# Attention and SwiGLU on one core: q, k and x turned on TensorE in all eight batches, stores issued from ScalarE's queue

## The chip, the core and the metric

The program runs on one core of one Trainium2 chip. The metric is the device time in microseconds (us); the lower the better. Five engines run beside each other, each through its own list of instructions in order: PE (TensorE, matrix products and transposes), DVE (VectorE), ACT (ScalarE), POOL (GpSimd) and SP (SyncE, which here only issues transfers). ACT and POOL can issue transfers too. DMA engines move the data.

## What is computed

For 8 batches with 8 heads, 576 tokens and head dimension 64, causal attention with a decay from a "forget" input f, and then an RMS norm and a SwiGLU feed-forward network over the 4608 tokens:

```
scores = q @ k.T / sqrt(64) + cum[:, None] - cum[None, :]      # cum = cumsum(log(clip(f)))
attn   = softmax(causal(scores));   x = attn @ v               # x: 4608 x 512, all heads side by side
xn     = x / sqrt(mean(x*x) + 1e-6) * rms_g
out    = (silu(xn @ w_gate) * (xn @ w_val)) @ w_out            # 512 -> 1536 -> 512
```

All inputs and the output are float32; the kernel works on bf16 copies of the matrix operands.

## The kernel before

**Attention, batch by batch.** TensorE needs q and k with the head dimension on the partitions, so each batch first has its rows turned. SP loads float32 pieces into staging buffers `st` (ten of them), POOL (for k of batch 0, DVE) casts them to bf16 (`ld`, six buffers), and then there are two ways. Batches listed in `PE_TURN`, here 0 and 1, load q and k as runs of four tokens (`load_runs`, 1 KB each), and PE turns them with an identity matrix (`turn`, 8 transposes for a pair of heads into one PSUM buffer `ff`; `turn_tail` for the last 64 tokens); DVE then copies the turned q and ACT the turned k into `QK` (`keep`). The other six batches load rows of 64 values, 256 bytes each (`load_rows`), and SP issues transposing transfers from `ld` to `QK` (`turn_dma`, 8 a batch, `turn_tail_dma` 1). The rows of v are loaded by SP in both ways and scaled by POOL into `Vs`.

Scores go into `sc` buffers, ACT takes the exponential into `PT`, POOL masks the diagonal blocks, PE multiplies with `Vs` (into `po` or `ff`), and DVE divides into `x`. ACT squares and sums x, POOL makes the factor `rs`, DVE makes `xn`. Then x is turned as well: by PE and a copy (`turn_x`, `keep_xt`) in the batches of `PE_TURN`, by SP's transposing transfers (`turn_x_dma`) in the others. The result is `xT`.

**FFN, group by group.** Two groups of 256 tokens and eight of 512. For each of 12 slices, PE makes the gate product and the value product (four matmuls each, into `ff`), ACT takes tanh, DVE does two operations. After the slices, PE makes the projections, twelve matmuls for 128 tokens, ACT copies each into `ores` (three buffers), and SP stores it (`store`).

**The three `ff` buffers** are shared by gate, value and projection, by the products with `Vs` that found `po` taken, and by all turning on PE.

**The order.** `Plan` holds every piece of work with its engine, an assumed duration, what it needs, and the buffers that it takes and gives back. `Plan.run` plays the pieces through with these durations, picks on each engine the ready piece of the best priority (on PE, attention or FFN by the share of each that is done), and the program is written out in that order. So each engine's order is fixed when the program is built, and the assumed durations and priorities decide it. At run time an engine waits wherever its next instruction is not ready.

Of the kernel before, what the change touches and what calls it, by code (L numbers as in the profile page):

```python
# [19 lines left out]
NP = H // 2  # L20

LEAD, UNTIL = 30.0, 0.74
Q_AHEAD, V_AHEAD, T_AHEAD = 1.6, 0.9, 0.95
SPLIT, PE_TURN = (0,), (0, 1)
GROUPS = ((0, 256), (256, 512)) + tuple((a, a + 512) for a in range(512, B * S, 512))
N_ST, N_LD, N_PT, N_XN = 10, 6, 4, 5
SV_PRIO = -0.7
# [25 lines left out]
class Plan:  # L53
# [20 lines left out]
    def run(self):  # L74
# [10 lines left out]
        free_at = dict.fromkeys(self.ENGINES, 0.0)  # L85
# [25 lines left out]
        while n_left:  # L111
            moved = False
            for e in self.ENGINES:
                if free_at[e] > t + 1e-9:
                    continue
                c = [p for p in ready[e] if can(p, t)]
                if not c:
                    continue
                if e == "PE":
                    behind = a_done < self.lead + (a_total - self.lead) * min(1.0, f_done / (f_total * self.until))  # L120
                    first = "A" if behind else "F"
                    p = min(c, key=lambda p: (p.kind != first, p.prio))
                    if p.kind == "A":
                        a_done += p.dur
                    else:
                        f_done += p.dur
                else:
                    p = min(c, key=lambda p: p.prio)
                ready[e].remove(p)
                if p.seq is not None:  # L130
                    next_seq += 1
                p.start, p.end = t, t + p.dur
                free_at[e] = p.end
                if p.xfer is None:
# [62 lines left out]
def kernel(  # L197
# [55 lines left out]
        for t in P4:  # L253
            nc.vector.memset(t[:, 256:], 0.0)

    clear = plan.add("clear", "DVE", 1.9, clear_early, prio=(-2,))
# [56 lines left out]
    p_scan = plan.add("scan", "DVE", 1.75, scan, [p_log], prio=(-3,))  # L313
# [45 lines left out]
    def attention(b):  # L359
# [9 lines left out]
        def load_rows(nm, src, j):  # L369
            nc.sync.dma_start(out=stage((nm + "s", b, j)).rearrange("p (h d) -> p h d", d=D),  # L370
                              in_=src[b, :, j * 128:(j + 1) * 128, :].rearrange("h p d -> p h d"))

        def load_runs(nm, src, pp):
            nc.sync.dma_start(out=stage((nm + "s", b, pp)).rearrange("p (h c) -> p h c", h=2),
                              in_=src[b, 2 * pp:2 * pp + 2, 0:512, :].rearrange("h (p i) d -> p h (i d)", i=4))
# [33 lines left out]
        for u in range(4):  # L409
            for nm, src in (("k", k), ("q", q)):  # L410
                key = f"{nm}{b}.{u}"
                fn = load_runs if pe else load_rows
# [3 lines left out]
                ld[nm, u] = plan.add("C" + key, eng, 0.36 if eng == "DVE" else 0.62,  # L416
                                     lambda nm=nm, u=u, eng=eng: cast((nm + "s", b, u), (nm, b, u), eng, pe), [a],
                                     acq=[("ld", key)], rel=["s" + key], prio=(ahead + 0.01 * u,))
        key = f"qk{b}"
# [5 lines left out]
        for j in range(NB):  # L425
            key = f"v{b}.{j}"
            late = (0.2 if j > 1 else 0.0) if split else 0.0
            vp = (b - V_AHEAD if not pe else b - 2.9) + 0.01 * j + late
            if j < 4:
                lv[j] = [plan.add("L" + key, "SP", 0.6, lambda j=j: load_rows("v", v, j), acq=[("st", "s" + key), ("hw", "h" + key)],  # L430
                                  rel=["h" + key], xfer=1.2, prio=(vp,), seq=True)]
            else:
                lv[j] = [plan.add(f"L{key}{par}", "SP", 0.45, lambda par=par: load_v4(par),
                                  acq=[("st", "s" + key), ("hw", f"h{key}{par}")], rel=[f"h{key}{par}"], xfer=0.4,
                                  prio=(vp,), seq=True) for par in range(2)]
            eng = "DVE" if b == 0 else "POOL"
            sv[j] = plan.add("S" + key, eng, (0.85 if j < 4 else 1.1) if eng == "DVE" else 1.35 if j < 4 else 1.9, lambda j=j, eng=eng: scale_v(j, eng),
                             lv[j] + [p_dec, clear] + old.get("val", []), rel=["s" + key],
                             prio=(1, b, -0.5) if eng == "DVE" else (b + SV_PRIO + 0.01 * j + late,))
        if b == 0:  # L440
# [4 lines left out]
        if pe:  # L445
# [5 lines left out]
                        nc.tensor.transpose(ps[:, t * 512 + u * 128:t * 512 + u * 128 + 128], x[:, u * 128:u * 128 + 128], ident)  # L451

            def keep(pp, t, eng):
                src = T["tr", b, pp][:, t * 512:t * 512 + 512].rearrange("p (i m) -> p i m", i=4)
                dst = QK[i][:, pp, t, :].rearrange("p (m i) -> p i m", i=4)
                (nc.vector.tensor_copy if eng == "DVE" else nc.scalar.copy)(dst, src)

            def turn_tail():
# [48 lines left out]
        def diag_k():  # L507
            for par in range(2):
                r = slice(par * 64, par * 64 + 64)
                nc.gpsimd.tensor_copy(K4[i][r, :, par * 64:par * 64 + 64], QT[i][r, :, 1, :])  # L510

        k4 = plan.add(f"k4.{b}", "POOL", 0.7, diag_k, [clear] + list({id(x): x for x in (tq["k", p, 4] for p in range(NP))}.values())
                      + old.get("sc4", []), prio=(b - 3 if pe else b - 0.01,))

        def scores4():
# [8 lines left out]
        def mask4():  # L524
# [8 lines left out]
        m4 = plan.add(f"mask4.{b}", "POOL", 0.5, mask4, [e, p_tri], prio=(b - 3,))  # L533
# [117 lines left out]
        def part(banks, qis, late):  # L651
# [29 lines left out]
            for h in range(0, H, step):  # L681
# [14 lines left out]
            rs = plan.add(f"rs{b}.{js[0]}", "POOL", 1.4, lambda: rstd(js), sq, prio=(bb - 4,))  # L696
            for j in js:
                xn = plan.add(f"xn{b}.{j}", "DVE", 0.65, lambda j=j: norm(js, j), [rs, p_rg], acq=[("xn", f"xn{b}.{j}")],
                              rel=[f"x{b}"], prio=(2, bb, j))
                if pe:  # L700
                    key = f"xtr{b}.{j}"
# [26 lines left out]
    def ffn(g):  # L728
# [33 lines left out]
            nc.scalar.copy(o, T.pop(("pj", g, j)))  # L762

        def store(j):
            nc.sync.dma_start(out=out[t0 + j * 128:t0 + (j + 1) * 128, :], in_=T.pop(("o", g, j)))

        last = None
        for fc in range(NFC):
# [13 lines left out]
        for j in range(w // 128):  # L782
# [44 lines left out]
```

## Time and profile before

| | us |
|---|---|
| median of three runs (437.78 to 438.83) | 438.27 |
| the profiled execution | 436.98 |
| its span, first to last instruction | 435.2 |
| PE busy | 373.9 (86%) |
| DVE busy | 247.5 (57%) |
| ACT busy | 220.8 (51%) |
| POOL busy | 159.8 (37%) |

The mean granted PE clock is 0.975 of full speed. 54.03 MB are moved in 155,847 packets. How to read the rows that follow: in a row of waits stand the engine and line that waited, the releaser, the microseconds in total, the number of waits, and the longest. "SPq" is SP's own list of transfers to issue; the time of such a row is that of the issuing, not that of the transfer. In a timeline row, brackets give the idle time of the engine ahead of it and what ended it. `x8` means eight instructions drawn together.

### The profile page before, as it was taken

What the parts mean: (1) busy time and instruction counts of PE and PEld (TensorE: products, weight loads), DVE (VectorE), ACT (ScalarE), POOL (GpSimd) and SP (SyncE); (2) the same over time, 40 slices, a digit from 0 to 9 for tenths busy, and PEclk for the clock granted to TensorE, in tenths of its full rate; (3) what the DMA queues carried; (4) which work ended last, traced back from release to release, by engine and by line L of the source; (5) the groups of instructions that cost most, each with busy time, mean ns of one, the idle gap of its engine ahead of it and who ended that gap; (6) DMA issues with size and microseconds to landing.
All of it is one profiled execution on the core that took longest, in us unless ns stands there. A gap on an engine that the chain in (4) does not pass through costs nothing.

```text
span 435.2 us, 8110 instructions
## 1 busy us (share of the span) xinstructions
PE 373.9 (86%) x3085; PEld 194.2 (45%) x3085; DVE 247.5 (57%) x462; ACT 220.8 (51%) x361; POOL 159.8 (37%) x259
## 2 busy tenths in 40 slices
PE   1557789899787859898598996899999999999996
PEld 1335665745344434453243442444445444444442
DVE  4774773766647127860776248533792774770760
ACT  2847686547575538536346266145662553332331
POOL 3497256467377328516623743401130111000000
PEclk9999999999998969999799999899999999999999
DMA  7999992589899489749967996201022002201002
GB/s 236 201 283 197 197 190 67 111 174 234 128 187 176 106 196 214 106 86 182 246 98 151 208 213 127 50 24 74 2 49 80 26 0 63 90 2 72 24 2 96
DMA packets 155847, 54.03 MB, mean 124 GB/s; under 512 B 141280, under 2 KB 151008, under 8 KB 155808
## 3 DMA queue, kind: packets, MB, share of 16 engines
q1 hardware_dynamic: 150016, 48.80, 55.1%
q0 software_dynamic: 5792, 4.72, 6.7%
q8 instruction: 24, 0.39, 0.4%
q14 instruction: 15, 0.12, 0.1%
HBM read 38.16 MB, written 9.44 MB: 109 GB/s over the span
## 4 chain that ended last, share of the span: by engine, by line
PE 40%; DMA 5%; SPq 4%; POOL 4%; DVE 2%; ACT 1%; issue 1%; POOLq 0%; ACTq 0%
PE ff L736 22%; PE ff L757 14%; DMA st<-in_v_dram 3%; SPq L482 3%; DMA QK<-ld 2%; PE po L585 2%; PE sc L550 1%; POOL Vs L398 1%; DVE xn L615 1%; POOL ld L391 1%; POOL PT L566 1%; ACT junk L602 1%; SPq L485 1%; POOL rs L611 1%; ACT th L741 1%
## 5 line engine op out<-in xcount | busy, mean ns | idle before, releaser
L736 PE MATMUL ff<-xT,wg 128*128 128x512 bf16 (+1 forms) x480 | 116.3, 366 | 4.7 <-ACT ores L762 4.0
L736 PE MATMUL ff<-xT,wv 128*128 128x512 bf16 (+1 forms) x480 | 115.3, 363 | 3.5 <-DVE ga L745 2.5
L558 ACT ACTIVATE PT<-sc 128x1024 bf16<-128x1024 f32 (+2 forms) x100 | 96.1, 993 | 31.8 <-PE sc L550 26.9
L745 DVE SCALAR_TENSOR_TENSOR ga<-th,ff 128x512 f32<-128x512 f32 (+1 forms) x120 | 75.7, 631 | 58.3 <-ACT th L741 58.1
L741 ACT ACTIVATE th<-ff 128x512 f32<-128x512 f32 (+1 forms) x120 | 66.4, 554 | 78.4 <-PE ff L736 77.7
L757 PE MATMUL ff<-wo,hT 128*128 128x512 bf16 x432 | 98.3, 381 | 0.0
L751 DVE SCALAR_TENSOR_TENSOR hT<-ga,ff 128x512 bf16<-128x512 f32 (+1 forms) x120 | 76.0, 633 | 18.0 <-PE ff L736 6.9
L566 POOL TENSOR_SCALAR_AFFINE_SELECT PT<-PT 128x1024 bf16<-128x1024 bf16 (+1 forms) x44 | 38.4, 883 | 86.3 <-ACT PT L558 86.0
L736 PEld LDWEIGHTS <-wg 128*128 128x128 bf16 x480 | 45.6, 99 | 52.1 <-issue 9.3
L736 PEld LDWEIGHTS <-wv 128*128 128x128 bf16 x480 | 45.2, 99 | 49.4 <-issue 10.1
L757 PEld LDWEIGHTS <-hT 128*128 128x128 bf16 x432 | 41.0, 98 | 48.4 <-issue 1.9
L762 ACT COPY ores<-ff 128x512 f32<-128x512 f32 x36 | 21.1, 586 | 80.2 <-PE ff L757 69.5
L391 POOL CAST ld<-st 128x512 bf16<-128x512 f32 x68 | 43.9, 671 | 24.4 <-DMA QK<-ld 13.1
L585 PEld LDWEIGHTS <-PT 128*128 128x128 bf16 x896 | 35.4, 101 | 28.9 <-POOL PT L566 18.4
L615 DVE SCALAR_TENSOR_TENSOR xn<-x,rs,rgb 128x512 bf16<-128x512 f32 x40 | 33.9, 879 | 19.6 <-POOL rs L611 19.5
L594 DVE RECIPROCAL rden<-po 128x5 f32<-128x5 f32 (+2 forms) x42 | 8.0, 191 | 60.5 <-PE po L585 59.9
L398 POOL TENSOR_TENSOR Vs<-st,decT 128x512 bf16<-128x512 f32 x28 | 30.5, 1089 | 27.3 <-DMA st<-in_v_dram 23.2
L550 PE MATMUL sc<-QK 64*128 64x128 bf16 (+2 forms) x328 | 31.1, 291 | 10.6 <-DMA QK<-ld 8.5
L585 PE MATMUL po<-Vs,PT 128*128 128x65 bf16 x563 | 26.0, 198 | 14.2 <-POOL PT L566 12.4
L550 PEld LDWEIGHTS <-QK 64*128 64x128 bf16 x584 | 17.1, 98 | 32.4 <-issue 25.4
L602 ACT ACTIVATE junk<-x 128x512 bf16<-128x512 f32 x40 | 25.1, 628 | 4.9 <-DVE x L595 4.3
L595 DVE TENSOR_TENSOR x<-po,rden 128x320 f32<-128x320 f32 (+2 forms) x42 | 20.1, 479 | 1.5
(65 smaller groups left out, 197.6 us busy)
## 6 DMA issues: line engine op xcount, KB each, us to landing
out_dram<-ores SPq DMA_DIRECT2D x36, 256.0 KB, 2.3
st<-in_k_dram SPq DMA_DIRECT2D x32, 256.0 KB, 5.0
st<-in_q_dram SPq DMA_DIRECT2D x32, 256.0 KB, 5.2
st<-in_v_dram SPq DMA_DIRECT2D x32, 256.0 KB, 4.9
wo<-in_moe_w_out_dram POOLq DMA_DIRECT2D x2, 768.0 KB, 15.8
st<-in_q_dram SPq DMA_DIRECT2D x8, 128.0 KB, 5.5
st<-in_k_dram SPq DMA_DIRECT2D x8, 128.0 KB, 5.2
st<-in_v_dram SPq DMA_DIRECT2D x16, 64.0 KB, 4.2
```

Of the source, the lines that this page charges most:

```text
L391: (nc.vector if eng == "DVE" else nc.gpsimd).tensor_copy(o, x)
L398: e.tensor_tensor(Vs[i][:, j, :, 0:D], t, bcast(dj, D), ALU.mult)
L550: nc.tensor.matmul(sc[:, par, c:c + n], lhsT=k_cols(r, p, kj), rhs=q_cols(r, p, q0, n), start=True, stop=True)
L558: nc.scalar.activation(T["pt", b, p][:, :, c0:c0 + n], T.pop(("sc", b, p, c0))[:, :, 0:n], ACT.Exp, scale=scale)
L566: nc.gpsimd.affine_select(out=d, in_=d, pattern=[[0, m], [1, 128]], compare_op=ALU.is_ge, fill=0.0, base=0, channel_multiplier=-1)
L585: nc.tensor.matmul(T["po", b, hs][:, qm, m, :], lhsT=w, rhs=Vs[i][:, kj, h, :], start=(kj == 0), stop=(kj == qi))
L615: nc.vector.scalar_tensor_tensor(xn, in0=T["x", b][:, j, :], scalar=T["rs", b, js][:, j:j + 1], in1=rgb, op0=ALU.mult, op1=ALU.mult)
L736: nc.tensor.matmul(ps[:, 0:w], lhsT=wt[:, dc, fc * 128:(fc + 1) * 128], rhs=T["xT", g][:, dc, 0:w], start=(dc == 0), stop=(dc == NDC - 1))
L741: nc.scalar.activation(t[:, 0:w], T["pg", g, fc][:, 0:w], ACT.Tanh, scale=0.5)
L745: nc.vector.scalar_tensor_tensor(a[:, 0:w], in0=T.pop(("th", g, fc))[:, 0:w], scalar=1.0, in1=T.pop(("pg", g, fc))[:, 0:w], op0=ALU.add, o ...
L751: nc.vector.scalar_tensor_tensor(T["hT", g][:, fc, 0:w], in0=T.pop(("ga", g, fc))[:, 0:w], scalar=0.5, in1=T.pop(("pv", g, fc))[:, 0:w], o ...
L757: nc.tensor.matmul(po, lhsT=T["hT", g][:, fc, j * 128:(j + 1) * 128], rhs=wo[:, fc, :], start=(fc == 0), stop=(fc == NFC - 1))
```

## The change

All eight batches are now in `PE_TURN`: q and k are loaded as 1 KB runs and turned on PE, x is turned on PE, and no transposing transfer is left. A store is issued by ACT, behind the copy that made its data, instead of by SP. The `keep` copies walk the same elements in another order: before, they read PSUM in sequence and wrote every fourth element of `QK`; now they write `QK` in sequence and read PSUM with a step of 128 elements. In the planner, the transfers' assumed start is later, SP is held up once its transfers in flight exceed a depth ("ring back-pressure"), and some assumed durations differ; these change the order only. The function `load_cast` and the branch that uses it are new, but with every batch in `PE_TURN` neither is reached.

```diff
-SPLIT, PE_TURN = (0,), (0, 1)
+SPLIT, PE_TURN = (0,), tuple(range(8))
...
                 else:
-                    dma_free = max(dma_free, p.start + 0.4 * p.dur) + p.xfer
+                    dma_free = max(dma_free, p.start + 0.7) + p.xfer
+                    if e == "SP":
+                        p.end = free_at[e] = max(p.end, dma_free - 2.0)
                     p.done = max(dma_free, p.end) + 1.7
...
-    p_two = plan.add("twice", "DVE", 0.12, twice, [p_exp], prio=(-3,))
+    p_two = plan.add("twice", "DVE", 0.6, twice, [p_exp], prio=(-3,))
...
             def keep(pp, t, eng):
-                src = T["tr", b, pp][:, t * 512:t * 512 + 512].rearrange("p (i m) -> p i m", i=4)
-                dst = QK[i][:, pp, t, :].rearrange("p (m i) -> p i m", i=4)
+                src = T["tr", b, pp][:, t * 512:t * 512 + 512].rearrange("p (i m) -> p m i", i=4)
+                dst = QK[i][:, pp, t, :].rearrange("p (m i) -> p m i", i=4)
                 (nc.vector.tensor_copy if eng == "DVE" else nc.scalar.copy)(dst, src)
...
         def store(j):
-            nc.sync.dma_start(out=out[t0 + j * 128:t0 + (j + 1) * 128, :], in_=T.pop(("o", g, j)))
+            nc.scalar.dma_start(out=out[t0 + j * 128:t0 + (j + 1) * 128, :], in_=T.pop(("o", g, j)))
...
-            plan.add("s" + ko, "SP", 0.45, lambda j=j: store(j), [c], acq=[("hw", "s" + ko)], rel=["s" + ko, ko], xfer=0.7,
-                     prio=(-1, g, j))
+            plan.add("s" + ko, "ACT", 0.45, lambda j=j: store(j), [c], acq=[("hw", "s" + ko)], rel=["s" + ko, ko], xfer=0.7,
+                     prio=(1.5, g, j))
```

The lists become, in rows: SP 175 to 100, ACT 208 to 291, DVE 448 to 486, POOL 195 in both, PE 6163 to 6835 (336 transposes, each with its weight load).

SP's list before, where the x of batch 4 and the q and k of batch 6 are turned, with the last loads of batch 6 ahead (L370 is `load_rows`, L378 `load_tail`, L765 the store, L634 `turn_x_dma`, L482 `turn_dma`):

```order
L765 DMA out_dram<-ores 128x512
L370 DMA st<-in_k_dram 128x8x64
L370 DMA st<-in_q_dram 128x8x64
L378 DMA st<-in_q_dram 64x8x64
L765 DMA out_dram<-ores 128x512
L378 DMA st<-in_k_dram 64x8x64
L765 DMA out_dram<-ores 128x512
L634 DMA_TRANSPOSE xT<-xn 128x4x128 x2
L765 DMA out_dram<-ores 128x512
L634 DMA_TRANSPOSE xT<-xn 128x4x128 x2
L634 DMA_TRANSPOSE xT<-xn 128x4x64
L482 DMA_TRANSPOSE QK_112<-ld 128x4x128 x8
```

And now, from the last loads of q and k of batch 6 to those of batch 7 (L381 is `load_runs`, L385 `load_tail`, L372 and L389 load v):

```order
L381 DMA st<-in_k_dram 128x2x256
L381 DMA st<-in_q_dram 128x2x256
L385 DMA st<-in_q_dram 64x8x64
L385 DMA st<-in_k_dram 64x8x64
L372 DMA st<-in_v_dram 128x8x64 x4
L389 DMA st<-in_v_dram 64x4x64 x2
L381 DMA st<-in_k_dram 128x2x256
```

Stores and transposes are gone from SP's list; what is left are loads, in the order of the batches.

DVE's list before, where `xn` of batch 4 is made (L594 and L595 divide into `x`, L615 is `norm`, L745 and L751 are the FFN's two operations):

```order
L594 RECIPROCAL rden<-po 128x5
L595 TENSOR_TENSOR x<-po,rden 128x5x64
L615 SCALAR_TENSOR_TENSOR xn<-x,rs,rgb 128x512 x5
L745 SCALAR_TENSOR_TENSOR ga<-th,ff 128x512
L751 SCALAR_TENSOR_TENSOR hT<-ga,ff 128x512
```

And now at that place (L476 is `keep_tail` of batch 5, L626 `norm` of batch 4, L467 `keep` of batch 6, L756 and L762 the FFN, L658 `keep_xt`):

```order
L476 COPY QT_115<-ff 128x512
L626 SCALAR_TENSOR_TENSOR xn<-x,rs,rgb 128x512
L467 COPY QK_112<-ff 128x512
L756 SCALAR_TENSOR_TENSOR ga<-th,ff 128x512
L762 SCALAR_TENSOR_TENSOR hT<-ga,ff 128x512
L626 SCALAR_TENSOR_TENSOR xn<-x,rs,rgb 128x512 x2
L756 SCALAR_TENSOR_TENSOR ga<-th,ff 128x512
L762 SCALAR_TENSOR_TENSOR hT<-ga,ff 128x512
L756 SCALAR_TENSOR_TENSOR ga<-th,ff 128x512
L762 SCALAR_TENSOR_TENSOR hT<-ga,ff 128x512
L658 COPY xT<-ff 128x4x128
L626 SCALAR_TENSOR_TENSOR xn<-x,rs,rgb 128x512 x2
```

The copies that turning on PE needs stand between the FFN's operations, and the five `norm` operations are spread out.

ACT's list now, where the projections of a group are copied and stored (L773 is `keep_o`, L776 the store, L569 the exponential, L660 `keep_xt`, L467 `keep`):

```order
L773 COPY ores<-ff 128x512
L660 COPY xT<-ff 128x4x128
L776 DMA out_dram<-ores 128x512
L569 ACTIVATE PT<-sc 128x2x512
L467 COPY QK_113<-ff 128x512
L569 ACTIVATE PT<-sc 128x2x512
L773 COPY ores<-ff 128x512
L776 DMA out_dram<-ores 128x512
```

Each store stands on ACT right behind the copy that it needs, or one instruction later.

More of the change, by code (lines that the diff above doesn't have):

```diff
@@ L254, in clear_early @@
             nc.vector.memset(t[:, 256:], 0.0)
-    clear = plan.add("clear", "DVE", 1.9, clear_early, prio=(-2,))
+    clear = plan.add("clear", "DVE", 1.75, clear_early, prio=(-2,))
     def load_f():
@@ L371, in load_rows, with load_cast @@
                               in_=src[b, :, j * 128:(j + 1) * 128, :].rearrange("h p d -> p h d"))
+        def load_cast(nm, src, j):
+            t = T[nm, b, j] = ldp.tile([128, H * D], BF16, name="ld", tag="ld")
+            nc.gpsimd.dma_start(out=t.rearrange("p (h d) -> p h d", d=D),
+                                in_=src[b, :, j * 128:(j + 1) * 128, :].rearrange("h p d -> p h d"))
         def load_runs(nm, src, pp):
@@ L411, in attention @@
                 key = f"{nm}{b}.{u}"
+                if not pe and nm == "k":
+                    ld[nm, u] = plan.add("L" + key, "POOL", 0.9, lambda nm=nm, src=src, u=u: load_cast(nm, src, u), xfer=2.1,
+                                         acq=[("ld", key), ("sw", "h" + key)], rel=["h" + key], prio=(ahead + 0.01 * u,), seq=True)
+                    continue
                 fn = load_runs if pe else load_rows
@@ L415, in attention @@
                 eng = "DVE" if b == 0 and nm == "k" else "POOL"
-                ld[nm, u] = plan.add("C" + key, eng, 0.36 if eng == "DVE" else 0.62,
+                ld[nm, u] = plan.add("C" + key, eng, 0.55 if eng == "DVE" else 0.62,
                                      lambda nm=nm, u=u, eng=eng: cast((nm + "s", b, u), (nm, b, u), eng, pe), [a],
@@ L436, in attention @@
             eng = "DVE" if b == 0 else "POOL"
-            sv[j] = plan.add("S" + key, eng, (0.85 if j < 4 else 1.1) if eng == "DVE" else 1.35 if j < 4 else 1.9, lambda j=j, eng=eng: scale_v(j, eng),
+            sv[j] = plan.add("S" + key, eng, (1.0 if j < 4 else 1.6) if eng == "DVE" else 1.35 if j < 4 else 1.9, lambda j=j, eng=eng: scale_v(j, eng),
                              lv[j] + [p_dec, clear] + old.get("val", []), rel=["s" + key],
@@ L510, in diag_k @@
                 nc.gpsimd.tensor_copy(K4[i][r, :, par * 64:par * 64 + 64], QT[i][r, :, 1, :])
-        k4 = plan.add(f"k4.{b}", "POOL", 0.7, diag_k, [clear] + list({id(x): x for x in (tq["k", p, 4] for p in range(NP))}.values())
+        k4 = plan.add(f"k4.{b}", "POOL", 0.85, diag_k, [clear] + list({id(x): x for x in (tq["k", p, 4] for p in range(NP))}.values())
                       + old.get("sc4", []), prio=(b - 3 if pe else b - 0.01,))
@@ L532, in attention @@
                      prio=(2, b + (0.05 if split else 0), -1))
-        m4 = plan.add(f"mask4.{b}", "POOL", 0.5, mask4, [e, p_tri], prio=(b - 3,))
+        m4 = plan.add(f"mask4.{b}", "POOL", 0.7, mask4, [e, p_tri], prio=(b - 3,))
         parts = ((HEAD, (0, 1)), (REST, (2, 3, 4))) if split else ((WHOLE, (0, 1, 2, 3, 4)),)
@@ L695, in part @@
                   for m, j in enumerate(js)]
-            rs = plan.add(f"rs{b}.{js[0]}", "POOL", 1.4, lambda: rstd(js), sq, prio=(bb - 4,))
+            rs = plan.add(f"rs{b}.{js[0]}", "POOL", 1.45, lambda: rstd(js), sq, prio=(bb - 4,))
             for j in js:
-                xn = plan.add(f"xn{b}.{j}", "DVE", 0.65, lambda j=j: norm(js, j), [rs, p_rg], acq=[("xn", f"xn{b}.{j}")],
+                xn = plan.add(f"xn{b}.{j}", "DVE", 0.75, lambda j=j: norm(js, j), [rs, p_rg], acq=[("xn", f"xn{b}.{j}")],
                               rel=[f"x{b}"], prio=(2, bb, j))
```

2 lines of the change are left out of this document (1 added, 1 removed).

## The prediction

> **What bounds the kernel now.** I read the page's first part, then the busy time by stages, then the waits from 50 to 280 us, then the timeline at the longest of them.
>
> ```profile
> PE 373.9 (86%) x3085; PEld 194.2 (45%) x3085; DVE 247.5 (57%) x462; ACT 220.8 (51%) x361; POOL 159.8 (37%) x259
> ...
> 0.00:50.00 50.00, 25.78 (x277) 17.66 (x278) 31.67 (x64) 29.04 (x38) 29.34 (x58) 1.00 1.14 225
> 50.00:280.00 230.00, 196.81 (x1851) 105.51 (x1848) 129.88 (x258) 126.87 (x215) 120.10 (x190) 0.96 0.84 157
> 280.00:358.00 78.00, 77.87 (x626) 38.07 (x625) 47.91 (x86) 40.46 (x65) 8.99 (x9) 1.00 0.11 36
> 358.00:431.50 73.50, 73.44 (x340) 33.02 (x338) 38.01 (x56) 23.80 (x44) 1.36 (x2) 1.00 0.15 48
> ```
>
> PE carries the time. After the window and its length come the busy times of PE, weight loads, DVE, ACT and POOL, then the clock, the DMA share and GB/s. From 280 us PE never rests, with attention mixed in up to 358. Its idle time lies in the head (24 us) and between 50 and 280 (33 us). The waits behind the second (engine, releaser, us in total, times, longest):
>
> ```profile
> POOL K L510 <- DMA QT<-ld: 27.2, 4, 10.5
> POOL Vs L398 <- DMA st<-in_v_dram: 23.2, 13, 6.7
> POOL ld L391 <- DMA QK<-ld: 13.1, 4, 5.8
> PE po L585 <- POOL PT L566: 11.6, 6, 3.8
> ACT ores L762 <- DMA out_dram<-ores: 9.7, 2, 6.5
> PE sc L550 <- DMA QK<-ld: 8.5, 2, 6.0
> PE ff L736 <- ACT ores L762: 4.3, 2, 4.0
> PE sc L518 <- POOL K L510: 2.0, 1, 2.0
> ```
>
> The four PE rows add up to 26.4 us. One waits for turned q and k itself. Two wait for POOL, whose own longest waits are for transfers: POOL takes its list in order, so a mask (L566) stands behind a scale of v or a cast that waits for a load or a free buffer. The last waits for ACT, and ACT for a store. All lead to SP's list:
>
> ```profile
> 152.97 2.52 SPq L482 DMA_TRANSPOSE QK<-ld  x2
> ...
> 156.21 1.23 SPq L485 DMA_TRANSPOSE QT<-ld  x1
> 156.84 1.05 PE L550 MATMUL sc<-QK 64*128 64x128 bf16 x8 [5.97 <-DMA QK<-ld]
> ...
> 205.64 1.31 SPq L370 DMA_DIRECT2D st<-in_q_dram  x1
> 207.05 1.09 SPq L765 DMA_DIRECT2D out_dram<-ores  x1
> 211.52 0.59 ACT L762 COPY ores<-ff 128x512 f32<-128x512 f32 x1 [6.51 <-DMA out_dram<-ores]
> 212.16 1.73 PE L736 MATMUL ff<-xT,wg 128*128 128x512 bf16 x4 [3.99 <-ACT ores L762]
> ```
>
> At 157 us SP had issued transposes back to back, 1.2 us each, and PE stood 5.97 us. At 207 a store goes out behind loads; the next copy finds no free `ores` buffer, holds its `ff` buffer, and PE stands 3.99 us. The four matmuls at 212 then took 1.73 us: the clock had dropped.
>
> **The change, step by step**, against the profiled execution's 436.98 us.
>
> *Transposing transfers and stores leave SP.* Gone are its 87 transposes, these 48 of q and k among them, and the stores:
>
> ```profile
> L482 SPq DMA_TRANSPOSE QK<-ld x48: 1188/1217/2791, 74.7 to 265.6; - x48
> L765 SPq DMA_DIRECT2D out_dram<-ores x36: 332/447/1516, 73.5 to 432.1; - x36
> ```
>
> At the median of 1.217 us the 87 were 106 us of SP's list, the stores 16 us more. SP then issues only loads, 16 a batch, as far ahead as ten `st` buffers allow, so v no longer stands behind nine transposes. Of the 26.4 us I take 24 as gone; masks can still be late behind casts, now more of them waiting ahead. The ends are 13 (POOL stays late half the time) and 26.4.
>
> *The clock.* Four of the five windows of 10 us in which it was below full (the fifth, at 0.94, is left out):
>
> ```profile
> 130.00:140.00 10.00, 7.66 (x76) 4.07 (x75) 7.52 (x13) 4.88 (x8) 7.74 (x11) 0.83 1.26 184
> 150.00:160.00 10.00, 4.03 (x26) 1.73 (x24) 0.00 (x0) 1.86 (x3) 1.88 (x3) 0.72 0.59 143
> ...
> 210.00:220.00 10.00, 6.88 (x56) 3.40 (x56) 8.96 (x13) 4.28 (x6) 4.66 (x5) 0.66 1.06 228
> 270.00:280.00 10.00, 6.68 (x49) 3.21 (x50) 4.82 (x10) 2.21 (x4) 5.92 (x10) 0.83 0.38 73
> ```
>
> Each holds or follows one of the long waits. PE's busy time times the missing clock is 7.66 x 0.17 + 4.03 x 0.28 + 6.88 x 0.34 + 6.68 x 0.17 = 5.9 us. I take 6; the ends are 2 (half the waits stay, and with them the drops) and 9 (the drop counted over whole windows, idle time too).
>
> *PE gets 336 transposes*: per batch 32 for q and k, 4 for the tail, 20 for x, six batches.
>
> ```profile
> 92.79 0.61 PE L640 MATMUL ff<-ident,xn 128*128 128x128 bf16 x8
> 93.24 0.28 PE L518 MATMUL sc<-QT,K 128*128 128x64 bf16 x4
> ...
> 59.91 0.40 PE L640 MATMUL ff<-ident,xn 128*128 128x128 bf16 x4
> 60.35 0.60 PE L736 MATMUL ff<-xT,wg 128*128 128x256 bf16 x4
> 61.90 0.27 PE L640 MATMUL ff<-ident,xn 64*128 64x64 bf16 x4 [0.51 <-DVE ga L745]
> ```
>
> Eight took 0.45 us to the next instruction, 0.056 each: +18.8 us. PE had no slack after 280 and should have little before, so all of it lies on the path.
>
> *New waits.* Each of 60 visits (24 pairs, 6 tails, 30 pieces of x) takes one of three `ff` buffers until a copy on DVE or ACT has emptied it. At 59.91 four transposes were followed after 0.44 us instead of 0.22; at 61.90 the visit waited 0.51 us for the FFN's DVE work. From nothing (scores and products with `Vs` are often ready, and need other buffers) to 0.44 a visit, 26 us. I take 0.15, nearer to nothing, because the order puts most visits beside such pieces: +9.
>
> *The `keep` copies*, 24 more on DVE and on ACT:
>
> ```profile
> L456 DVE COPY QK<-ff 128x512 bf16<-128x512 bf16 x8 | 10.4, 1296 | 9.8 <-PE ff L451 6.0 <-ACT QK L456 3.8
> L456 ACT COPY QK<-ff 128x512 bf16<-128x512 bf16 x8 | 10.2, 1311 | 9.7 <-PE ff L451 5.2 <-DVE QK L456 3.8 <-DVE rden L594 0.6
> L465 DVE COPY QT<-ff 128x512 bf16<-128x512 bf16 x2 | 0.8, 418 | 0.6 <-PE ff L462 0.6
> L649 ACT COPY xT<-ff 128x512 bf16<-128x512 bf16 (+1 forms) x5 | 2.4, 502 | 0.3 <-PE ff L640 0.3
> ```
>
> The same 512 elements cost 1.30 us with a stepped write, on both engines although they differ elsewhere (next two rows), and 0.42 to 0.6 in sequence. That points to the write, which the new order makes sequential; the stepped PSUM read that it brings appears in no row of this size. I take 0.6, with 0.42 and 1.3 as ends. At 0.6 DVE gets 24 x 0.6, six tails and 18 or so pieces of x at 0.42, together 24 us; ACT 24 x 0.6, about 15 pieces at 0.6 and the 28 stores ahead of the last two groups at 0.45, 36 us. Between 50 and 358 us they are busy 178 and 167 of 308 us, so both rise to about two thirds: cover enough, as from 280 to 358 where DVE's 48 of 78 us cost PE nothing. If the cover is gone, the price is that of the third rival.
>
> The Trainium skill speaks against this step: "Advanced Engine Details and Errata", Memory Cachelines, gives SBUF 16-byte and PSUM 8-byte lines and wants at least two hits on a line. By it the old write (two elements a line) should have been cheap and the new read (one a line) dear; with copies still at 1.3 the sum would be the third rival's. The 1.296 us against 0.418 contradict its first half; no row here tests the second.
>
> *Stores on ACT.* A store costs SP 0.45 us of issuing; on ACT it also waits until the copy ahead of it is finished. ACT's next work, a tanh or exponential, waits as long, and PE for that only if its `ff` or `sc` buffers run out. I count nothing in the late part (ACT busy 23.8 of 73.5 us) and leave the early part within the new waits. The gain, `ores` freed in time, is in the 26.4.
>
> *The head.* Batch 1's turning used to stand in PE's list ahead of the first FFN work, and PE waited there for casts:
>
> ```profile
> 30.38 1.03 PE L451 MATMUL ff<-ident,ld 128*128 128x128 bf16 x8 [1.40 <-POOL ld L391]
> 37.18 1.03 PE L451 MATMUL ff<-ident,ld 128*128 128x128 bf16 x8 [1.04 <-POOL ld L391]
> ```
>
> Now it comes after most of the first group's FFN. These 2.4 us should go, and the eight copies of batch 0 shorten the way to the first exponential; against that, POOL issues four weight loads ahead of batch 0's `rs`. I take -4, ends -8 and +3.
>
> *Short losses.* Counted from PE's order, what it did from 50 to 280 is 364 gate or value and 192 projection matmuls of 512 columns, 168 of 256, 678 products with `Vs`, 33 visits of scores and some 40 small ones. At the spacing of the undisturbed part,
>
> ```profile
> 340.11 0.55 PE sc L550 x14
> 343.81 2.59 PE ff L736 x12
> 346.40 0.46 PE po L585 x15
> ```
>
> that is 556 x 0.216 + 168 x 0.108 (half the columns) + 678 x 0.0307 + 33 x 0.55 + 3 = 180 us. PE was busy 196.8; 5.9 of the difference is the clock, some 11 are short stalls and drains. At worst all stay; with the long waits gone I take half as gone, -5.
>
> Sum: 436.98 - 24 - 6 + 18.8 + 9 - 4 - 5 = 425.8 us. The profiled execution stands 1.3 us below the median of the runs, so on the median's scale 427.
>
> **The rivals.** *The mixed part becomes as dense as 280 to 358 is now*: all 26.4 us of waits go, 9 of the short losses, the new waits cost 3, the head gives 5: 427 - 2.4 - 4 - 6 - 1 = 414. For it: PE idled 0.13 us in those 78. Against: no turning happens there.
>
> *POOL stays the last releaser*: it still has 120 us of work in 230, in order, and its casts wait for loads. Then 12 more of the waits stay, 3 of the clock and the 5 short ones: 447, slower. Against: its longest waits name transposes or loads behind them. No gain is left once some 9 of the 26.4 us stay.
>
> *The copies stay at 1.3 us*, by the stepped PSUM read: each of 24 visits holds its `ff` buffer 0.7 us longer and takes DVE and ACT from the FFN, +17 us if PE has nothing else: 444, slower than before. It turns the sign from 0.47 us a visit. The rows leave the stepped read open, but the equal 1.30 on two engines points at the write, so I give it 0.13. (The rule of the Trainium skill, "Advanced Engine Details and Errata", Memory Cachelines, would make it so.)
>
> *Stores hold up ACT*: 28 x 0.55 us, all on the path, 15 us: 442. Against: ACT has a third of its time free, and stores leave it time after the copy.
>
> **How the numbers follow.** Forecast 0.48 (its own range 419 to 435), dense 0.22, POOL late 0.10, copies slow 0.13, stores 0.07. The time is the first's, 427. The range, 410 to 445, cuts off half of the dense case's lower spread and the worst of the slow ones. Within 0.2% (about what a measurement here tells from no change) of 438.27 fall the forecast's upper end and parts of the slow cases: 0.05. Slower: most of POOL late and copies slow, a part of stores: 0.21. Faster: 0.74.
>
> **What the profile would show.** Right: no wait of PE or POOL for QK, QT or `ores` transfers; the keep copies near 0.6; a clock of 1.00 between 50 and 350; PE busy near 382 with about 3420 matmuls. Wrong: keep rows at 1.3; PE rows "ff <- DVE" or "<- ACT" beyond 20 us; PE still waiting for PT masks for 10 us.

## The result, and the profile after

| | before | after |
|---|---|---|
| median of the runs, us | 438.08 (437.78 to 438.83) | 428.14 (426.66 to 428.72) |
| ratio, 95% interval | | 0.9765 [0.9738, 0.9793] |
| span of the profiled execution | 435.2 | 426.5 |
| PE busy in it | 373.9 | 385.9 |
| PE idle in it (span less busy) | 61.3 | 40.6 |

The changed kernel is 2.3% faster, and 428 us stand where 427 were forecast. PE works 12.0 us longer and idles 20.7 us less. The profile's first part, and the busy time by stages (window and length, then PE, weight loads, DVE, ACT and POOL, the clock, the DMA share, GB/s), of the kernel after:

```profile
PE 385.9 (90%) x3421; PEld 211.2 (50%) x3421; DVE 262.4 (62%) x512; ACT 235.6 (55%) x398; POOL 160.1 (38%) x259
...
0.00:50.00 50.00, 29.52 (x329) 21.01 (x330) 30.08 (x80) 25.60 (x46) 27.81 (x54) 1.00 1.14 222
50.00:280.00 230.00, 215.66 (x2145) 122.28 (x2146) 148.01 (x290) 147.39 (x245) 120.67 (x193) 1.00 0.46 120
280.00:350.00 70.00, 68.69 (x607) 35.41 (x606) 47.89 (x88) 40.59 (x70) 11.56 (x13) 1.00 0.06 21
350.00:426.50 76.50, 72.02 (x344) 32.47 (x341) 36.38 (x56) 22.02 (x38) 0.00 (x0) 1.00 0.11 42
```

Idle time fell where it was: in the head from 24.2 to 20.5 us, from 50 to 280 us from 33.2 to 14.3. The clock is 1.00 throughout this execution, where it was 0.96 in the mixed stage, and the DMA engines are half as busy there (0.46 for 0.84). The last window takes in the 3.7 us behind PE's last matmul; from 280 us up to that matmul (at 422.8) PE idles 2.1 us, where before it idled 0.2. Waits of the kernel after from 50 to 280 us (engine, releaser, us in total, times, longest):

```profile
POOL PT L577 <- ACT PT L569: 54.9, 12, 10.5
...
POOL Vs L405 <- PE po L596: 19.1, 2, 13.2
...
ACT ores L773 <- DMA out_dram<-ores: 6.0, 3, 2.0
...
POOL Vs L405 <- DMA st<-in_v_dram: 3.4, 1, 3.4
PE ff L747 <- DVE ga L756: 3.0, 5, 0.8
```

PE no longer waits here for a transfer of q and k or for `ores`, and for a mask once, 0.7 us; its longest row is five short waits for the FFN's `ga`. POOL, which waited 63.5 us for transfers (QT, v, QK), now waits for ACT's exponentials and for PE: it is early where it was late. `ores` still holds ACT up in three waits of at most 2.0 us, which cost PE nothing that its waits show.

The groups of instructions, by shape, of the kernel after (times in all, mean ns of one, idle time ahead and what ended it):

```profile
L467 DVE COPY QK<-ff 128x512 bf16<-128x512 bf16 x32 | 21.5, 688 | 19.5 <-PE ff L462 16.1 <-ACT QK L467 3.2
...
L467 ACT COPY QK<-ff 128x512 bf16<-128x512 bf16 x32 | 18.6, 585 | 16.9 <-DVE QK L467 10.4 <-PE ff L462 6.4
...
L660 ACT COPY xT<-ff 128x512 bf16<-128x512 bf16 x14 | 8.2, 587 | 1.8 <-PE ff L651 1.8
L658 DVE COPY xT<-ff 128x512 bf16<-128x512 bf16 x14 | 5.7, 414 | 0.0
```

The `keep` copies went from 1.30 us to 0.69 on DVE and 0.585 on ACT. The stores of the kernel after, their issuing on ACT (ns: least, median, most; first and last start in us):

```profile
L776 ACTq DMA_DIRECT2D out_dram<-ores x36: 338/338/376, 61.5 to 423.5; - x36
```

The first store starts 12 us earlier than before (61.5 for 73.5), and issuing one takes 338 ns at the median against 447 on SP.

### The profile page after: what moved, and what is told of

The parts are those of the page before. It is cut to its first block, busy times and chain, and to the rows that moved or that the text cites. A ratio compares the mean times of both kernels' runs of the same rounds, so it can differ in the third digit from the quotient of the medians.

```text
span 426.5 us, 8697 instructions
## 1 busy us (share of the span) xinstructions
PE 385.9 (90%) x3421; PEld 211.2 (50%) x3421; DVE 262.4 (62%) x512; ACT 235.6 (55%) x398; POOL 160.1 (38%) x259
## 4 chain that ended last, share of the span: by engine, by line
PE 64%; DVE 13%; ACT 11%; POOL 7%; issue 3%; DMA 1%; POOLq 0%; SPq 0%; DVEq 0%
PE ff L747 31%; PE ff L768 20%; ACT junk L613 4%; PE sc L561 4%; DVE xn L626 3%; PE po L596 3%; DVE ga L756 3%; PE ff L462 2%; DVE QK L467 2%; ACT th L752 2%; DVE hT L762 2%; ACT QK L467 2%; POOL PT L577 2%; POOL ld L398 2%; DVE x L606 1%
## 5 line engine op out<-in xcount | busy, mean ns | idle before, releaser
L747 PE MATMUL ff<-xT,wv 128*128 128x512 bf16 (+1 forms) x480 | 113.9, 360 | 4.3 <-DVE ga L756 1.8
L747 PE MATMUL ff<-xT,wg 128*128 128x512 bf16 (+1 forms) x480 | 114.1, 361 | 3.2 <-DVE ga L756 1.3
L569 ACT ACTIVATE PT<-sc 128x1024 bf16<-128x1024 f32 (+2 forms) x100 | 95.8, 989 | 25.8 <-PE sc L561 24.3
L756 DVE SCALAR_TENSOR_TENSOR ga<-th,ff 128x512 f32<-128x512 f32 (+1 forms) x120 | 75.7, 631 | 53.2 <-ACT th L752 52.8
L762 DVE SCALAR_TENSOR_TENSOR hT<-ga,ff 128x512 bf16<-128x512 f32 (+1 forms) x120 | 76.1, 634 | 17.9 <-PE ff L747 7.7
L398 POOL CAST ld<-st 128x512 bf16<-128x512 f32 x68 | 42.8, 658 | 29.2 <-PE ff L473 8.4
L773 ACT COPY ores<-ff 128x512 f32<-128x512 f32 x36 | 21.1, 586 | 57.5 <-PE ff L768 49.5
L596 PEld LDWEIGHTS <-PT 128*128 128x128 bf16 x896 | 33.9, 98 | 9.2 <-POOL PT L577 1.0
L405 POOL TENSOR_TENSOR Vs<-st,decT 128x512 bf16<-128x512 f32 x28 | 29.3, 1046 | 22.6 <-PE po L596 19.1
L626 DVE SCALAR_TENSOR_TENSOR xn<-x,rs,rgb 128x512 bf16<-128x512 f32 x40 | 33.4, 865 | 6.0 <-POOL rs L622 6.0
L467 DVE COPY QK<-ff 128x512 bf16<-128x512 bf16 x32 | 21.5, 688 | 19.5 <-PE ff L462 16.1
L462 PE MATMUL ff<-ident,ld 128*128 128x128 bf16 x256 | 20.4, 231 | 11.8 <-DVE mid L280 9.5
L467 ACT COPY QK<-ff 128x512 bf16<-128x512 bf16 x32 | 18.6, 585 | 16.9 <-DVE QK L467 10.4
L561 PEld LDWEIGHTS <-QK 64*128 64x128 bf16 x584 | 17.0, 97 | 20.5 <-issue 14.4
```

Of the source, the lines that this page charges most:

```text
L398: (nc.vector if eng == "DVE" else nc.gpsimd).tensor_copy(o, x)
L561: nc.tensor.matmul(sc[:, par, c:c + n], lhsT=k_cols(r, p, kj), rhs=q_cols(r, p, q0, n), start=True, stop=True)
L569: nc.scalar.activation(T["pt", b, p][:, :, c0:c0 + n], T.pop(("sc", b, p, c0))[:, :, 0:n], ACT.Exp, scale=scale)
L596: nc.tensor.matmul(T["po", b, hs][:, qm, m, :], lhsT=w, rhs=Vs[i][:, kj, h, :], start=(kj == 0), stop=(kj == qi))
L626: nc.vector.scalar_tensor_tensor(xn, in0=T["x", b][:, j, :], scalar=T["rs", b, js][:, j:j + 1], in1=rgb, op0=ALU.mult, op1=ALU.mult)
L747: nc.tensor.matmul(ps[:, 0:w], lhsT=wt[:, dc, fc * 128:(fc + 1) * 128], rhs=T["xT", g][:, dc, 0:w], start=(dc == 0), stop=(dc == NDC - 1))
```

## Experiments

A ratio is to the kernel before, run beside it on the same chip. Beside these runs the kernel before had medians from 436.25 to 439.06 us, so a difference of 2 or 3 us between kernels of different chips is better read from the ratios.

| kernel | us, median | ratio [95%] |
|---|---|---|
| after | 428.14 | 0.9765 [0.9738, 0.9793] |
| a_oldkeep | 456.14 | 1.0396 [1.0352, 1.044] |
| a_spstore | 431.97 | 0.9847 [0.9811, 0.9883] |
| a_oldplan | 427.49 | 0.9742 [0.9711, 0.9772] |
| a_turn2x | 440.17 | 1.0045 [1.0024, 1.0066] |
| b_newkeep | 433.46 | 0.9875 [0.982, 0.9931] |
| b_actstore | 432.80 | 0.9886 [0.9832, 0.994] |
| c_both | 429.39 | 0.9785 [0.9729, 0.9841] |
| a_qk_dma | 421.03 | 0.961 [0.9573, 0.9647] |
| a_x_dma | 414.55 | 0.9466 [0.9421, 0.9511] |
| c_x_dummy | 425.13 | 0.9687 [0.9652, 0.9722] |
| c_qkhalf | 405.84 | 0.9251 [0.9212, 0.929] |
| d_qkhalf_sp | 404.93 | 0.9264 [0.9193, 0.9334] |

**One part undone, or doubled.** Four kernels made from the one after.

a_oldkeep, the `keep` copies walk as before:

```diff
-src = T["tr", b, pp][:, t * 512:t * 512 + 512].rearrange("p (i m) -> p m i", i=4)
-dst = QK[i][:, pp, t, :].rearrange("p (m i) -> p m i", i=4)
+src = T["tr", b, pp][:, t * 512:t * 512 + 512].rearrange("p (i m) -> p i m", i=4)
+dst = QK[i][:, pp, t, :].rearrange("p (m i) -> p i m", i=4)
```

> The changed kernel (428.1 us) with the keep copies walking as before: PSUM read in sequence, QK written with a step of four; the order on every engine is unchanged. The forecast's third rival as a measurement: if PE has nothing else to do while a copy holds its ff buffer, 24 visits at 0.7 us more give +17 us, 445 us, and the DVE and ACT rows of L467 stand at 1.30 us. If scores, products with Vs and other FFN work cover the longer copies, as they cover most of the new waits, it stays within +4 us, up to 432.

456.14 us, 28.0 over the kernel after. Groups of a_oldkeep from 50 to 280 us, and its longest PE wait:

```profile
L467 ACT COPY QK<-ff 128x512 bf16<-128x512 bf16 x24 | 30.6, 1302 | 15.0 <-DVE QK L467 14.3 <-PE ff L462 0.6
L467 DVE COPY QK<-ff 128x512 bf16<-128x512 bf16 x24 | 30.3, 1310 | 13.7 <-PE ff L462 11.1 <-ACT QK L467 2.5
```

```profile
PE ff L747 <- ACT QK L467: 11.6, 9, 2.0
```

The copies are at 1.30 us again, the next gate or value product waits 11.6 us for a `ff` buffer. Both expectations (445, or up to 432) were too low. The clock has little part in it: it was 0.959 in this execution and 0.996 in another one, which still took 453.84 us. Without the new walk the rest of the change is slower than the kernel before.

a_spstore, stores issued and planned on SP:

```diff
-nc.scalar.dma_start(out=out[t0 + j * 128 ...
+nc.sync.dma_start(out=out[t0 + j * 128 ...
-plan.add("s" + ko, "ACT", 0.45, ..., prio=(1.5, g, j))
+plan.add("s" + ko, "SP", 0.45, ..., prio=(-1, g, j))
```

> The changed kernel with the stores back on SP's list, planned there as before (priority -1). Theory of the forecast: SP's list was what made things late, and a store behind a load that waits for a buffer leaves ores full; SP now waits for POOL in pieces of up to 28 us, so some stores are late and PE waits again: 431 to 438 us. Rival (it matters only that the transposing transfers left SP): 428, within 1 us.

431.97 us: stores on ACT are worth 3.8 us even when no transpose stands on SP. SP's own longest wait in a_spstore:

```profile
SPq L776 <- ACT ores L773: 232.2, 32, 32.2
```

SP stands at its stores for 232 us in all until ACT has made the data. Only the part ahead of the last load (251 us) can hold loads up; from 50 to 252 us it is

```profile
SPq L776 <- ACT ores L773: 68.3, 13, 23.0
```

and the loads listed behind such a store go out that much later.

a_oldplan, the planner's numbers of before:

```diff
-dma_free = max(dma_free, p.start + 0.7) + p.xfer      # and SP's hold-up, and durations
+dma_free = max(dma_free, p.start + 0.4 * p.dur) + p.xfer
```

> The changed kernel with the planner's assumed numbers of before (durations, start of a transfer, no ring back-pressure); all transposes on PE and stores on ACT as changed. Theory of the forecast (the gain is in the work taken off SP): 427 to 432 us. Rival (the gain is in the better planned order): 436 us or more.

427.49 us; the intervals overlap. The planner's changed numbers show no worth here.

a_turn2x, each of the 336 new transposes issued twice, into the same buffer:

```diff
-for u in range(4):
+for u in (0, 1, 2, 3) * (1 if b < 2 else 2):      # and likewise for the tail and for x
```

> The changed kernel with every transpose of batches 2 to 7 on PE issued twice into the same place, 336 more, each written with the same values; the order is otherwise the same. If the transposes lie on the path as the forecast's sum has them (0.056 us each), +18.8 us: 447 us. If PE's remaining idle time takes them, +5 or less: below 433.

440.17 us, 12.0 more, or 0.036 us a transpose, between the two expectations. The first part of its profile:

```profile
PE 402.7 (92%) x3757; PEld 228.8 (52%) x3757; DVE 262.9 (60%) x512; ACT 236.1 (54%) x398; POOL 160.5 (37%) x259
```

PE is busy 16.8 us longer than after, 0.050 each; 4.8 of it went into time in which PE had idled. This prices further transposes in a visit that is there already; a visit of its own costs more, as c_x_dummy shows.

**Parts alone on the kernel before.** b_newkeep has only the new walk, b_actstore only the stores on ACT (the same lines as above, the other way).

> The kernel before (438 us) with nothing but the new walk of the keep copies (16 copies, of batches 0 and 1); the order is unchanged. The first part of the forecast's term for the head: the copies of batch 0 lie on the way to the first exponential and those of batch 1 in front of the FFN, so 0.6 to 0.7 us less each gives 433 to 436 us. Rival (the head is set by the loads of batches 0 and 1, which are not changed): 437 to 439.

> The kernel before with nothing but the stores planned and issued on ACT. If the 4.3 us that PE waited for ores, and their part of the clock, were the stores' doing and nothing takes their place: 431 to 435 us. Rival (SP's transposes make everything late anyway, so the next wait grows by as much): 437 to 440.

433.46 and 432.80 us, 4.0 and 4.7 under their runs of before (437.45). Groups of b_newkeep:

```profile
L456 DVE COPY QK<-ff 128x512 bf16<-128x512 bf16 x8 | 5.5, 687 | 6.7 <-PE ff L451 4.8 <-ACT QK L456 2.0
L456 ACT COPY QK<-ff 128x512 bf16<-128x512 bf16 x8 | 4.7, 582 | 7.6 <-PE ff L451 5.2 <-DVE QK L456 2.5
```

Sixteen copies, all in batches 0 and 1, took 0.6 or 0.7 us less each; they lie in the head, and 4.0 of their some 10 us reach the time.

**Half of the transposes back on SP.** In the kernel after, x of batches 2 to 7 by SP's transposing transfers (a_x_dma), or q and k (a_qk_dma, with loads of rows as before):

```diff
 a_x_dma:    in the branch of x       -if pe:                                +if b < 2:
 a_qk_dma:   in attention()           -split, pe = b in SPLIT, b in PE_TURN  +split, pe = b in SPLIT, b < 2
             in the branch of x       -if pe:                                +if True:
             k loaded on SP           -if not pe and nm == "k":              +if False:
```

> The changed kernel, but x of batches 2 to 7 is turned by SP's transposing transfers as before (33 of them); q and k stay on PE. It takes 120 transposes off PE (about 4 us by what doubling all 336 cost, 12 us) and 30 copies off DVE and ACT. If any block of transposes on SP makes loads late: 432 us or more. If only those of q and k did, since nine of them stood ahead of each batch's v: 422 to 427, faster than the change.

> The other half: q and k of batches 2 to 7 loaded in rows of 256 bytes and turned by SP as before (54 transposes), x on PE. If those 54 in SP's list are what made PE wait, most of the loss is back: 434 to 442 us. If the stores and x were the larger part: below 430.

414.55 and 421.03 us: both halves beat the whole. a_x_dma is faster than either of its expectations, and for a_qk_dma the rival came true: with q and k back on SP, POOL waits 19.7 us for QT (27.2 before) but PE only 3.2 for masks and 2.0 for QK. So the whole move was tried the other way round.

**No transpose moved at all.** c_both is the kernel before with the new walk and the stores on ACT.

> The kernel before with the new walk of the keep copies and the stores on ACT's queue, and nothing else of the change: every transpose of q, k and x of batches 2 to 7 stays with SP's DMA. My forecast's theory (the long waits of PE go because the transposes leave SP's queue): the waits for PT and QK stay, so 428 to 431 us, little under b_newkeep (433.5) and b_actstore (432.8) alone. The theory that the queue was only too long while it held stores as well: with the stores gone the transposes do no more harm, both savings (4 and 5 us) come together and the 336 transposes cost PE nothing, 415 to 423 us, under the full change (428.1). If the halves' gains (414.6 with x on SP, 421.0 with q and k on SP) are those of half a load on each of SP and PE, this end has SP overfull again and lies above 424.

429.39 us (four runs, 427.18 to 436.94; 428.77 without the longest), as far as these can tell the time of the full change, and what my theory gave (428 to 431), though only one of its two waits stayed. Waits of c_both from 50 to 280 us, PE's and then POOL's:

```profile
PE po L585 <- POOL PT L566: 9.1, 6, 2.8
PE ff L736 <- DVE ga L745: 8.5, 5, 3.8
PE sc L518 <- ACT PT L558: 3.2, 1, 3.2
PE ff L736 <- ACT ores L762: 2.9, 1, 2.9
```

```profile
POOL PT L566 <- ACT PT L558: 33.5, 12, 7.5
POOL K L510 <- DMA QT<-ld: 21.8, 3, 8.2
POOL Vs L398 <- DMA st<-in_v_dram: 15.9, 10, 3.4
POOL ld L391 <- DMA QK<-ld: 9.3, 3, 4.0
```

POOL still waits 47.0 us for turned q and k and for v (63.5 before), and PE for masks 9.1 (11.6 before). The transposes on SP do hold this chain up, as the prediction read it; PE's wait for QK itself (8.5 before) is down to 0.4 though. The gain over before came from the walk and the stores, and what moving all the transposes saved in waits, their work on PE took back, as near as these runs can tell.

**What x costs on PE.** c_x_dummy is a_x_dma with PE also turning x of batches 2 to 7 into a `ff` buffer that nobody reads:

```diff
+plan.add(key, "PE", 0.23, lambda j=j: turn_x(j), [xn], acq=[("ff", key)], rel=[key, f"xn{b}.{j}"],
+         prio=(bb, -1, j), kind="A")
```

> a_x_dma (414.6 us) with the 120 transposes of x of batches 2 to 7 also issued on PE into a ff buffer that nobody reads; xT still comes from SP's DMA transposes, no copy is added. It splits the 13.6 us between a_x_dma and the full change into PE's part and the rest. If PE's own time is what x costs: 120 x 0.036 (from a_turn2x) to 120 x 0.056 = 4 to 7 us, plus some waits for xn and for the ff buffer, so 420 to 423. If it is the order in which PE waits for xn and takes a ff buffer that costs, the whole of it: 425 to 428. If it is the 30 copies on DVE and ACT and the wait of the FFN for them: 415 to 418.

425.13 us, 10.6 of the 13.6 us between a_x_dma and after: 0.35 us for each of 30 visits without any copy. Its four transposes at 0.036 are 0.14 of that; the other 0.21 is what a visit costs, with all that comes with it: the wait for `xn`, the `ff` buffer, and the other order that the planner makes with 30 more pieces (a_turn2x keeps the order). These three were not separated. That is the lower end of what the visits alone were to cost (425 to 428); PE's own time by itself (4 to 7 us, to 423) is too little, and the copies, for which 415 to 418 stood, are the last 3.0 us. The clock is not the reason: in the profiled execution it was 0.66 from 20 to 40 us, but the run with a mean clock of 1.000 took 425.40 us, no less.

**Early and late batches.** c_qkhalf is a_x_dma with q and k of batches 5 to 7 on SP as well. It holds a second edit that its expectation does not name: with these batches out of PE's way of turning, `load_cast` came alive and took their k on POOL's transfers. d_qkhalf_sp takes that away:

```diff
 c_qkhalf:       -split, pe = b in SPLIT, b in PE_TURN   +split, pe = b in SPLIT, b < 5
 d_qkhalf_sp:    the same, and  -if not pe and nm == "k":   +if False:
```

> a_x_dma (414.6 us: x of batches 2 to 7 by SP's DMA transposes, q and k on PE) with q and k of batches 5 to 7 on SP as well (3 x 36 transposes less on PE, 3 x 9 copies less on DVE and ACT, 27 more DMA transposes on SP). If PE's work is what bounds it from here: 108 x 0.036 to 0.056 less, 409 to 412 us. If SP's queue of transposes holds the loads up again as soon as q and k are in it: 416 to 424, with PE waits for QK from DMA.

> c_qkhalf (405.8 us) with the k of batches 5 to 7 loaded on SP as in the kernel before, and cast on POOL: c_qkhalf had these 12 blocks loaded and cast by DMAs of POOL's queue, a second edit that I had not named. If c_qkhalf's gain over a_x_dma (414.6) is that 108 transposes and 27 copies are off PE, DVE and ACT while SP has room by then: 405 to 409 us. If the gain is that POOL has 12 casts less (12 x 0.65 = 7.8 us of POOL) and SP 12 loads less, and the transposes of these batches on SP bring nothing: 411 to 415. If SP's queue fills again: PE waits for QK from DMA and the time is above 415.

405.84 and 404.93 us: `load_cast` makes no difference that shows, the gain is over the 3 to 6 us that PE's part was to give, and these two, the fastest of the study, are 7.4 to 7.5% faster than before. The first parts of the profiles of a_x_dma and of d_qkhalf_sp:

```profile
PE 377.4 (91%) x3301; PEld 205.1 (50%) x3301; DVE 256.3 (62%) x492; ACT 230.2 (56%) x385; POOL 158.6 (38%) x259
```

```profile
PE 369.7 (92%) x3193; PEld 197.0 (49%) x3193; DVE 248.4 (62%) x477; ACT 222.8 (55%) x373; POOL 161.9 (40%) x259
```

Of the 9.9 us between their spans (413.4 and 403.5), PE's busy time makes 7.7, its idle time 2.2. From a_x_dma to after it is 8.5 us of busy time for the 120 transposes of x and 4.6 of idle time. Both are 0.071 us of busy time a transpose, more than the 0.050 of a_turn2x, where the visits were there already; so by the profile, in which the ends of matmuls are modelled, most of what these visits cost is PE being busy, the smaller part waiting.

The stretch from 170 to 230 us in the kernel after, in c_both and in d_qkhalf_sp:

```profile
170.00:230.00 60.00, 57.94 (x505) 30.51 (x504) 39.66 (x75) 33.59 (x54) 18.52 (x27) 1.00 0.21 64
```

```profile
170.00:230.00 60.00, 50.14 (x413) 24.23 (x420) 35.03 (x61) 29.99 (x48) 27.96 (x46) 0.97 0.81 153
```

```profile
110.00:170.00 60.00, 57.56 (x535) 29.16 (x532) 40.29 (x75) 40.78 (x67) 34.06 (x55) 1.00 0.72 144
170.00:230.00 60.00, 59.89 (x495) 29.16 (x494) 35.17 (x63) 33.40 (x53) 25.93 (x38) 1.00 0.90 157
```

After the full change the DMA engines stand at 0.21 while PE is full of transposes beside its products. With all transposes on SP the DMA is at 0.81 and PE has some 10 us idle (a few of its matmul records are missing there). In d_qkhalf_sp the DMA is at 0.90 and PE at 59.89 of 60: a busy DMA is no trouble by itself. SP issues the turning of batches 5, 6 and 7 in d_qkhalf_sp at

```profile
148.73 10.49 SPq L493 DMA_TRANSPOSE QK<-ld  x8
191.52 10.93 SPq L493 DMA_TRANSPOSE QK<-ld  x8
232.56 11.80 SPq L493 DMA_TRANSPOSE QK<-ld  x8
```

and in the kernel before from 174.09, 220.47 and 254.49 us, 22 to 29 us later. No wait of PE from 110 to 280 us names a transfer or POOL in d_qkhalf_sp, so this turning delays PE nowhere that shows. In d_qkhalf_sp POOL's wait for a QT transfer is gone from the mixed stage, and what is left of its waits for QK are ten short ones:

```profile
POOL ld L398 <- DMA QK<-ld: 6.0, 10, 1.2
```

The five kernels with the new walk and stores on ACT, by where the transposes of batches 2 to 7 are done:

| q and k | x on SP | x on PE |
|---|---|---|
| all on SP | 429.4 (c_both) | 421.0 (a_qk_dma) |
| batches 2 to 4 on PE, 5 to 7 on SP | 404.9 (d_qkhalf_sp) | not run |
| all on PE | 414.6 (a_x_dma) | 428.1 (after) |

Read downwards on the left: q and k of batches 2 to 4 on PE bring 24.5 us, those of 5 to 7 cost 9.6 (0.09 a transpose), and x then costs 13.6 (0.11 a transpose): together 1.3 us, less than the spread of c_both's runs. By the ratios the steps are 23, 9, 13 and 1 us. The same x brings 8.4 us when q and k all stand on SP. (c_both has the planner's old numbers; that they make no difference was run only on the kernel after.) The mirror image, q and k of batches 2 to 4 on SP and 5 to 7 on PE, was not run. So it is shown that moving three batches beats moving six or none; that it has to be the early three is not.

## Why the prediction was right, and which steps were not

The forecast of 427 us is 1 us from the measured 428, its working less near.

*Waits, -24.* Right in the trace: of the four PE rows, 26.4 us before, one wait of 0.7 us for a mask is left in the mixed stage. The chain SP, POOL, mask is shown by c_both, which keeps it, and a_x_dma, which has lost it. But the step gave transposes and stores one price. PE's wait for QK went from 8.5 to 2.1 us by the stores alone (b_actstore), and q and k of three batches bring more than those of six. Moving all 87 transfers was not needed for it.

*Clock, -6.* Right in the trace: no window of the stages is below 1.00. What it is worth is not shown: of the four runs of the kernel after, the one with a mean clock of 0.976 was the fastest (426.66 us). Nor do later runs tie a low clock to PE's waits alone: in the profiled executions of a_oldkeep and of a_oldplan, which took 456 and 428 us, it was 0.50 from 20 to 30 us.

*336 transposes, +18.8, and 60 visits, +9.* The sum was near, the split wrong. A further transpose in a visit costs 0.036 us on the path, not 0.056, so 12.0; a visit of x costs 0.21 us and not 0.15, which for 60 would be 12.6 (an estimate; those of q and k were not priced apart). In the waits of the mixed stage, PE's rows for `ff` behind DVE, or behind ACT's copies of turned k, rose from 5.0 to 10.9 us, 5.9 of the 9 forecast. For a visit of x the prediction's 4 x 0.056 + 0.15 = 0.37 stands against 0.35 measured, and 0.45 with the copies.

*Keep copies, 0.6.* Right: 0.585 on ACT, 0.688 on DVE. The rival's price was too low: +17 was forecast for slow copies, 28.0 were measured. Of these, 4.0 are the sixteen copies of the head (b_newkeep), which the +17 left out; the other 24 are then 1.0 us a visit instead of 0.7 (b_newkeep's figure is from the kernel before, so this split is an estimate). The Trainium skill's rule on lines of memory ("Advanced Engine Details and Errata", Memory Cachelines) is not borne out by these copies for SBUF, and for PSUM, where the page names matmuls, only on DVE: two elements on a 16-byte line of SBUF cost 1.30 us, one on an 8-byte line of PSUM 0.585 on ACT, as much as the copy in sequence (0.587), and 0.688 on DVE, where the copy in sequence took 0.414.

*Stores.* Counted at nothing, their gain put into the 24. They give 3.8 us in the kernel after and 4.7 alone. That is a step which the sum did not have by itself. ACT was not held up so that PE felt it: PE's waits for ACT in the mixed stage are 1.8 and 0.7 us, both for copies of turned k.

*Head, -4.* PE had done 3.7 us more work by 50 us (29.52 for 25.78), and its first FFN matmul came at 34.16 us instead of 38.01. The size is right, one of its two reasons is not. The 2.4 us of waits were to go because batch 1's turning no longer stands ahead of the FFN; but b_newkeep, which keeps that order and one wait of 1.48 us, starts the FFN earlier still:

```profile
26.70 1.03 PE L451 MATMUL ff<-ident,ld 128*128 128x128 bf16 x8 [1.48 <-POOL ld L391]
33.08 1.06 PE L736 MATMUL ff<-xT,wg 128*128 128x256 bf16 x4
```

```profile
34.16 1.01 PE L747 MATMUL ff<-xT,wg 128*128 128x256 bf16 x4 [0.67 <-ACT xT L660]
```

The first two rows are of b_newkeep, the third is of the kernel after. The shorter copies alone give the head its 4 us; with them the new order adds nothing that shows (with the long ones it does: a_oldkeep starts the FFN at 36.46 us).

*Short losses, -5.* Not separated by any run. PE's idle time outside the four rows went from 6.8 to 13.6 us in the mixed stage, but that holds the new waits too. This stays open; that the unproven 5 and the stores' 3.8 to 4.7, which have no term, are of one size is luck.

By its own terms the prediction made the transposes' move a near balance (-24 - 6 + 18.8 + 9 = -2.2, with the stores' part of the waits in it), and c_both to after is 1.3 us. What it did not see is that a part of the move brings far more than the whole: it took PE's waits as one sum for all six batches and the added work as another, and never asked how much of the work has to move before the waits go. That question finds the 23 us that the full change leaves on the table. The rows of before do not answer it by themselves: of the 26.4 us, 11.4 fall between 110 and 170 us, 8.7 from 170 to 230 and 6.3 after that, and in d_qkhalf_sp those of the later batches are gone too, though their q and k are still turned by SP. That SP, once late, stays late from batch to batch would fit this, and the earlier issues of d_qkhalf_sp as well; that it is not their mere number a_qk_dma suggests, which has fewer transposes on SP than d_qkhalf_sp (54 for 60) and takes 16 us longer, but its x stands on PE. The mirror image would decide it.

## What to carry to other kernels

When work is moved from a late engine to the one that bounds the kernel, price it piece by piece and try it in parts: here q and k of three batches of six on PE, and no x, beat the whole move and none by 23 to 25 us, because every piece that moves costs the bounding engine and the waits were gone before the last had moved. How busy the DMA engines are (0.90 in the fastest kernel) does not say whether a list is late; the waits of the engine behind it do. Issue a store where its data is made, not on a list with loads behind it.

## Hardware, as the runs showed it

- A bf16 copy of 128 x 512 that writes every fourth element of SBUF took 1.30 us on DVE and on ACT alike; the same elements read from PSUM with a step of 128 elements and written in sequence took 0.69 on DVE and 0.585 on ACT. Copies of that size in sequence on both sides took 0.414 and 0.587, so the stepped PSUM read cost DVE 0.27 us and ACT nothing that shows.
- A PE transpose of 128 x 128 cost 0.036 us of this kernel's time behind others of the same visit, and 0.09 (visit without copy) to 0.11 us (with it) when four come as a visit of their own.
- Issuing a store of 256 KB took 338 ns on ACT, nearly without spread, and 332 to 1516 ns on SP behind loads and transposes.
